# A state-space convolution with gated mixing: six additions moved from VectorE into accumulating transfers begun by GpSimd

## The chip, the cores and the metric

One Trainium2 chip, of which the kernel uses one core. A core has TensorE (PE in the profile; its weight loads are PEld), VectorE (DVE), ScalarE (ACT), GpSimd (POOL) and SyncE (SP), each with its own queue of instructions, worked off in order, and 16 DMA engines that all queues share. The metric is the device time of one launch in microseconds; lower is better. Inputs and the output are bfloat16, of 2048 rows and 512 channels.

## What is computed

The reference, cut to what matters:

```python
# A: a state-space convolution over L = 2048 positions, for each of 512 channels
dt = exp(log_dt); logdA = dt * (A_re + 1j*A_im)
P  = exp(logdA[:, :, None] * l)                    # 128 states, 2048 lags
K  = einsum("dn,dnl,dn->dl", C, P, dt*B).real      # kernel of lags
y  = irfft(rfft(pad(u)) * rfft(pad(K)))[:, :L] + u * Dskip
# B: two rows of x, chosen by the largest x @ w_r, go through a gated feed-forward
#    and are added back to those rows
b  = x + scatter(two rows, sigmoid(r) * ((silu(x_sel @ w_gate) * (x_sel @ w_up)) @ w_down))
# mix
g  = sigmoid((x * gate_w).sum(-1))
out = g * y + (1 - g) * b
```

## The kernel before

**Lags.** The kernel of lags needs exp(logdA * l) for 2048 lags. A lag is split into a coarse and a fine part, t1 + t2, and a table is built for each: the coarse table (`coarse`, tile TP: 32 lags, real and imaginary) and the fine table (`fine`, tiles X and Y in TQ: 20 lags and 8 more). Each is an exponential decay times a cosine or a sine of a phase; ScalarE makes the decays and the sines, VectorE multiplies. The channels are worked in two halves of 256, called half 0 and half 1. TensorE then sums over the states (`lags`: matmuls L889 and L890, evictions `kae`, a selection matmul L903, and the evictions `kce` and `kcx` into the tile KC).

**The fine table of one half** (`fine`, L840 to L859) goes through VectorE in steps of 2048 or 4096 columns per partition. For each of two groups of four lags: `px` (one product into X), `py` (the other product into a scratch tile `t4` at A+22528), `ps` (X += `t4`). Group k = 0 is lags 0 to 3, group k = 1 is lags 4 to 7. Then two wide products `px` and `py` for lags 8 to 15, from group 0, and for the last four lags again `px`, `py` into the same scratch place, `ps`. The scratch place `t4` is one range of bytes for all three sums of a half.

**Transforms.** The input U goes through a forward transform (`transform`, L729; TensorE L716) in two blocks m = 0, 1 of 1024 positions and two planes pl (real, imaginary). The matmuls of one tile first sum the odd rows, which are evicted doubled (`fwo`), then go on summing the even rows, so that the same bank then holds the sum of both (`fwe`). The difference, the spectrum's other half, is `fwe - fwo`: `vb` (L739), one VectorE operation of 2048 columns for each block and plane, four in all. The `vb` results are read only by the products of spectra (`products`, L952), late in the kernel.

**Spectra and inverse.** `spectrum` (TensorE L930, L932, L935) turns KC into the spectrum KH of the lag kernel, evicted by ScalarE (`khe`). `products` multiplies on VectorE, partly summed by TensorE (L993 to L997), and `inverse` (L1071, L1076) goes back to positions; evictions (L1087, L1091) scale by g, and the rows go out.

**The routed rows.** Beside all this, small steps (`rows`) find the two rows, gather them, run the feed-forward on TensorE (L779, L795 is the down projection `dn`, which reads `hh`, made by GpSimd) and scatter two rows into a copy of the input in DRAM (`sc`, L812, an indirect transfer begun by GpSimd, which needs `bu`). GpSimd also does the small steps of the gate: `sgd`, `sgo`, `gf`, `gc`, `omg`, and last `rr` (L814), which waits for the reciprocal `rrec` (L813) on VectorE. `rr` is read by `rd` (L1127): eight scalings of the identity matrix on ScalarE (L1131), used by the inverse for the share 1 - g.

**What sets the order.** Every step is an entry of a program (`Prog.add`) with its engine, the tiles it reads and writes, and a cost. `add` gives each step the steps it must wait for: the writers of what it reads, and the writers and readers of what it overwrites, in other tiles too that share bytes (`b.overlaps()`). The order is written out by hand in `PLAN`, a list of (step, engine choice); each engine's queue is that list with only its own steps. The costs play no part when the list is replayed. At run time a step waits on semaphores: one counter for each engine, and one of its own for each DMA, which reaches its count when the data has landed. A step that waits holds up everything behind it in its engine's queue.

**Names for the numbers of the list.** `vb`: 106 and 97 (block 0), 183 and 192 (block 1). Half 0's fine table: 258 `px`, 259 `py`, 260 `ps` (group k = 1), 263 `px`, 264 `py`, 265 `ps` (last four lags), 262 and 261 the wide products. Half 1's: 368 `px`, 369 `py`, 370 `ps` (k = 1), 373 `px`, 374 `py`, 375 `ps`, 372 and 371 wide; 367 is a sign change of half 1 (`nz`), 366 another (`nf`). 153 is `rrec`, 152 `sc`, 154 `rr`, 315 `rd`, 290 and 293 the evictions `kce`, 292 `kcx`, 144 `hh`.

VectorE's queue around them: 244, 245, 259, 367, 260, 264, 251, 265, 252, 261, then coarse steps of half 1, 363, 365, 153, 369, 373, 370, 290, 374, 366, 375, 372, 371, then 106, 97, the products of spectra with 183 and 192 among them. GpSimd's: 51, 77, 78, 84, 86, 55, 57, 58, 59, 80, 60, 82, 83, 140, 142, 143, 144, 152, 154. ScalarE's, late in the lags: 182 (`fwe` of block 1), 396, 286, 288, 315, 292, 293.

Of the kernel before, what the change touches and what calls it, by code (L numbers as in the profile page):

```python
# [15 lines left out]
ALU = mybir.AluOpType  # L16
# [290 lines left out]
def bass_gated_mix__ssm_conv_s4__moe_arch_mod__prompt_kernel(nc, A_u, A_A_re, A_A_im, A_B_re, A_B_im, A_C_re, A_C_im, A_log_dt, A_Dskip,  # L307
# [36 lines left out]
    with ExitStack() as es:  # L344
# [7 lines left out]
        P = Prog()  # L352
# [29 lines left out]
        def c_act(n):  # L382
            return 0.10 + n * 0.83e-3
# [17 lines left out]
        def f_act(o, a_, scale=1.0):  # L401
            return lambda h: h.activation(out=o(), in_=a_(), func=ACTF.Copy, scale=scale() if callable(scale) else scale)  # L402
# [12 lines left out]

        def DMA(name, fn, rd, wr, kb, n=1, eng=SP, issue=0.5, lat=2.2, **kw):
            return P.add(name, [(eng, issue, fn)], rd, wr, dma=(lat, kb / 270.0, n), **kw)

        def DMAT(name, o, a_, wr, kb, issue=1.25, lat=4.2, first=0.0):
            return P.add(name, [(SP, issue, lambda h: [h.dma_start_transpose(out=o(), in_=a_())])], [], wr, dma=(lat, kb / 250.0, 1), first=first)  # L420
# [288 lines left out]
        def forward(m, pl, kp, behind):  # L709
            t = P.pst(2, "fw", (0, 2))  # L710
            def product(par):
                def fw(h):
                    x = None
                    for k2 in range(2):
                        for i, (q, r) in enumerate((q, r) for q in range(2) for r in (par, par + 2)):
                            x = h.matmul(P32(t, k2, 0, 128, 0, (1, 512)), FM(0, 128, pl * 4096 + (par * 4 + i) * 512 + (2 * kp + k2) * 128, (1, 128)), U(0, 128, ((m * 2 + q) * 4 + r) * 512, (1, 512)),  # L716
                                         start=(par == 1 and i == 0), stop=(par == 0 and i == 3), skip_group_check=True)
                    return x
                MM("fw", fw, [bU[m][par], bF[pl]], [t], 1.73, behind=behind)
            def store(hc):  # L720
                o = lambda: V(0, 128, vo[m][2 * kp] + (hc * 2 + pl) * 512, (2048, 2), (1, 512))
                a = lambda: P32(t, 0, 0, 128, 0, (1, 1024))
                if hc == 0:
                    EV("fwe", o, a, [t], [bV[m][0][pl]], 1024)
                else:
                    P.add("fwo", [(ACT, c_act(1024), f_act(o, a, 2.0)), (DVE, c_dve(1024, 1), lambda h: h.tensor_scalar(out=o(), in0=a(), scalar1=2.0, scalar2=None, op0=ALU.mult))], [t], [bVO[m][pl]])  # L726
            return product, store

        def transform(m, behind=()):  # L729
            P.part = "transform%d" % m  # L730
            for pl in range(2):
                tiles = [forward(m, pl, kp, behind) for kp in range(2)]
                for hc in (1, 0):
                    for product, store in tiles:
                        product(hc)
                    for product, store in tiles:
                        store(hc)
                v = lambda hc, pl=pl: (lambda: V(0, 128, vo[m][0] + (hc * 2 + pl) * 512, (vo[m][2] - vo[m][0], 2), (2048, 2), (1, 512)))
                TT("vb", v(1), v(0), v(1), ALU.subtract, [bV[m][0][pl], bVO[m][pl]], [bV[m][1][pl]], 2048)  # L739
        transform(0)  # L740


# [97 lines left out]
        def fine(hf):  # L840
            P.part = "fine%d" % hf
            X, Y, Z, W, N, T = eX[hf], eY[hf], eZ[hf], eW[hf], eN[hf], el("A", 22528)
            bx = bX[hf]
            x = lambda j, n_, c=0, st=5120: ap(X + 5120 * c + 256 * j, (st, 2), (256, n_), (1, 256))
            t4 = ap(T, (1024, 2), (256, 4), (1, 256))
            for k, (j0, b0) in enumerate(((0, 4), (4, 0))):
                bt = bf_("t%d_%d" % (j0, hf), "A", 22528, 4096)
                TT("px", x(j0, 4), ap(W + 256, (256, 2), (0, 4), (1, 256)), ap(Z + 512 * b0, (0, 2), (512, 4), (1, 256)), ALU.mult, [bW[hf], bZ[hf][k]], [bx[k]], 2048)
                TT("py", t4, ap(W, (256, 2), (0, 4), (1, 256)), ap(Z + 512 * b0 + 256, (0, 2), (512, 4), (1, 256)), ALU.mult, [bW[hf], bZ[hf][k]], [bt], 2048)
                TT("ps", x(j0, 4), x(j0, 4), t4, ALU.add, [bx[k], bt], [bx[k]], 2048)  # L850
                if k == 0:
                    TS("nf", ap(N, (1, 256)), ap(X + 5120, (1, 256)), -1.0, ALU.mult, [bx[0]], [bNF[hf]], 256, 4)
                    TS("nz", ap(N + 256, (1, 256)), ap(Z + 512 * 8 + 256, (1, 256)), -1.0, ALU.mult, [bZ[hf][2]], [bNZ[hf]], 256, 4)
            TT("px", x(8, 8), ap(X, (5120, 2), (0, 8), (1, 256)), ap(Z, (0, 2), (512, 8), (1, 256)), ALU.mult, [bx[0]] + bZ[hf][:2], [bx[2]], 4096)
            TT("py", ap(Y, (2048, 2), (256, 8), (1, 256)), ap(N, (X - N, 2), (0, 8), (1, 256)), ap(Z + 256, (0, 2), (512, 8), (1, 256)), ALU.mult, [bx[0], bNF[hf]] + bZ[hf][:2], [bY[hf]], 4096)
            bt = bf_("t16_%d" % hf, "A", 22528, 4096)
            TT("px", x(16, 4), x(0, 4), ap(Z + 512 * 8, (0, 2), (0, 4), (1, 256)), ALU.mult, [bx[0], bZ[hf][2]], [bx[3]], 2048)
            TT("py", t4, x(0, 4, 1, -5120), ap(N + 256, (Z + 512 * 8 - N, 2), (0, 4), (1, 256)), ALU.mult, [bx[0], bNZ[hf], bZ[hf][2]], [bt], 2048)
            TT("ps", x(16, 4), x(16, 4), t4, ALU.add, [bx[3], bt], [bx[3]], 2048)  # L859
# [350 lines left out]
```

## Time and profile before

| | us |
|---|---|
| median of 3 runs (lowest to highest) | 158.67 (158.35 to 159.69) |
| the profiled execution's own time | 159.26 |
| its span, first to last instruction | 157.2 |
| TensorE busy (share of the span) | 140.8 (90%) |
| VectorE busy | 137.9 (88%) |
| ScalarE busy | 119.0 (76%) |
| GpSimd busy | 21.0 (13%) |

The span is what the trace covers; the execution's own time holds some 2 us around it. Busy times are unions of an engine's instructions; a matmul's end is modelled, so a busy TensorE is not one at its peak. The rows of a timeline give start, length, engine, line, operation, the tiles written and read, and their shapes; in brackets stands how long the engine was idle before and what ended the wait. All tiles in on-chip memory are views of one tensor, RB, and all banks are psm; most VectorE operations are recorded at the helper's line L386, so a step is told by its place in the queue and its size.

### The profile page before, as it was taken

To read this page: it belongs to the slowest core of one execution; us is meant where nothing else is said; L and a number is where in the kernel's file an instruction comes from. 1 tells how busy PE (TensorE), PEld (TensorE's weight loads), DVE (VectorE), ACT (ScalarE), POOL (GpSimd) and SP (SyncE) were. 2 spreads that over 40 slices of the span, in tenths; PEclk is the share of its full clock that TensorE was granted. 3 is DMA by queue.
4 is the path that set the end of the run, shared out by engine and by line. 5 is a ranking of instruction groups with operands and counts; after the bars stand their busy time and mean duration, and the time that the engine had idled before them with its cause. 6 is when DMAs were issued, how large, how long until landed. Compare 5 with 4: busy or idle time off the path is not lost.

```text
span 157.2 us, 3769 instructions
## 1 busy us (share of the span) xinstructions
PE 140.8 (90%) x1622; PEld 103.5 (66%) x1635; DVE 137.9 (88%) x184; ACT 119.0 (76%) x177; POOL 21.0 (13%) x26
## 2 busy tenths in 40 slices
PE   2479998999998999999967999999999999999960
PEld 0259976444764555778636899668877767777850
DVE  0799689999998999999999999999987999996930
ACT  5699999999999898887982754758687963567820
POOL 5000011564508800002020000000000000000000
PEclk9999999999999999999999999999999999999996
DMA  3999999968399000340397500558000040000157
GB/s 84 216 245 272 314 424 409 407 233 254 103 364 559 17 0 4 81 190 1 65 363 259 152 8 4 179 163 264 15 4 0 0 133 0 6 0 0 33 159 212
DMA packets 20932, 24.35 MB, mean 155 GB/s; under 512 B 9358, under 2 KB 18068, under 8 KB 20244
## 3 DMA queue, kind: packets, MB, share of 16 engines
q1 hardware_dynamic: 20642, 23.97, 47.3%
q8 instruction: 13, 0.21, 0.6%
q10 hardware_dynamic: 146, 0.13, 0.3%
q0 software_dynamic: 128, 0.01, 0.2%
q14 instruction: 3, 0.02, 0.0%
HBM read 19.78 MB, written 4.20 MB: 153 GB/s over the span
## 4 chain that ended last, share of the span: by engine, by line
PE 53%; DVE 32%; issue 4%; POOL 3%; ACT 2%; DMA 1%; POOLq 1%; ACTq 0%
DVE RB L386 23%; PE psm L930 9%; PE psm L1076 9%; PE psm L993 5%; PE psm L889 4%; PE psm L995 3%; PE psm L548 3%; PE psm L997 3%; PE psm L932 2%; PE psm L1071 2%; POOL RB L396 2%; PE psm L935 2%; DVE RB L726 2%; DVE RB L408 2%; PE psm L598 2%
## 5 line engine op out<-in xcount | busy, mean ns | idle before, releaser
L386 DVE TENSOR_TENSOR RB<-RB 128x2048 bf16<-128x2048 bf16 (+5 forms) x112 | 110.0, 1033 | 2.4 <-ACT RB L402 1.1
L402 ACT ACTIVATE RB<-psm 128x1024 bf16<-128x1024 f32 (+5 forms) x54 | 49.1, 945 | 23.7 <-PE psm L997 10.0
L716 PE MATMUL psm<-RB 128*128 128x512 bf16 x121 | 28.8, 379 | 1.2 <-ACT RB L402 0.5
L411 ACT ACTIVATE RB<-RB 128x512 bf16<-128x512 f32 (+6 forms) x48 | 27.0, 644 | 1.7 <-DVE RB L386 1.5
L411 ACT ACTIVATE RB<-psm 128x1024 bf16<-128x1024 int16 (+2 forms) x23 | 21.6, 968 | 2.5 <-DVE RB L386 1.2
L716 PEld LDWEIGHTS psm<-RB 128*128 128x128 bf16 x128 | 11.7, 97 | 14.0 <-ACT RB L402 1.1
L1076 PE MATMUL psm<-RB 128*128 128x256 bf16 x128 | 18.9, 273 | 0.0
L889 PE MATMUL psm<-RB 128*128 128x80 bf16 x256 | 16.5, 197 | 0.0
L890 PE MATMUL psm<-RB 128*128 128x32 bf16 x256 | 16.4, 177 | 0.0
L889 PEld LDWEIGHTS psm<-RB 128*128 128x128 bf16 x256 | 16.1, 96 | 0.2
L890 PEld LDWEIGHTS psm<-RB 128*128 128x128 bf16 x256 | 16.0, 96 | 0.2
L930 PE MATMUL psm<-RB 128*128 128x256 bf16 x128 | 14.5, 273 | 1.5 <-ACT RB L402 1.5
L930 PEld LDWEIGHTS psm<-RB 128*128 128x128 bf16 x128 | 12.4, 98 | 3.9 <-ACT RB L402 2.1
L1076 PEld LDWEIGHTS psm<-RB 128*128 128x128 bf16 x128 | 12.5, 98 | 1.5
L408 DVE CAST RB<-psm 128x1024 bf16<-128x1024 f32 (+3 forms) x8 | 8.6, 1080 | 3.7 <-PE psm L548 1.7
L993 PE MATMUL psm<-RB 128*128 128x512 bf16 x35 | 11.3, 379 | 0.3
L1087 ACT ACTIVATE RB<-psm,RB 128x256 bf16<-128x256 f32 x25 | 9.8, 477 | 1.3 <-PE psm L1076 1.1
L396 POOL CAST RB<-RB 128x16 bf16<-128x16 f32 (+4 forms) x6 | 7.2, 1197 | 24.8 <-DVE RB L405 16.9
L618 PE MATMUL psm<-RB 128*128 128x256 f16 x64 | 9.0, 272 | 0.0
L1071 PE MATMUL psm<-RB 128*128 128x256 bf16 x32 | 8.7, 273 | 0.0
L995 PE MATMUL psm<-RB 128*128 128x256 bf16 x40 | 8.3, 272 | 0.1
L997 PE MATMUL psm<-RB 128*128 128x256 bf16 x40 | 8.3, 273 | 0.0
(74 smaller groups left out, 156.9 us busy)
## 6 DMA issues: line engine op xcount, KB each, us to landing
RB<-c_fwd SPq DMA_DIRECT2D x2, 1024.0 KB, 7.9
RB<-in_A_u_dram SPq DMA_DIRECT2D x2, 1024.0 KB, 6.8
RB<-c_near SPq DMA_DIRECT2D x2, 1024.0 KB, 5.2
RB<-u_routed SPq DMA_DIRECT2D x2, 1024.0 KB, 5.1
RB<-in_B_w_up_dram SPq DMA_DIRECT2D x1, 1792.0 KB, 10.4
RB<-in_B_w_gate_dram SPq DMA_DIRECT2D x1, 1792.0 KB, 14.4
RB<-in_B_w_down_dram SPq DMA_DIRECT2D x1, 1792.0 KB, 8.7
out_dram<-RB SPq DMA_DIRECT2D x6, 256.0 KB, 3.0
```

The lines of the kernel that those rows point to most:

```text
L386: return P.add(name, [(eng, c_dve(n, mode) if eng == DVE else 1.6, lambda h: h.tensor_tensor(out=o(), in0=a_(), in1=b_(), op=op))], rd, wr ...
L402: return lambda h: h.activation(out=o(), in_=a_(), func=ACTF.Copy, scale=scale() if callable(scale) else scale)
L411: return P.add(name, [(ACT, cost or c_act(n), lambda h: h.activation(out=o(), in_=a_(), func=func, scale=scale))], rd, wr, table=table, **kw)
L716: x = h.matmul(P32(t, k2, 0, 128, 0, (1, 512)), FM(0, 128, pl * 4096 + (par * 4 + i) * 512 + (2 * kp + k2) * 128, (1, 128)), U(0, 128, ((m ...
L889: h.matmul(P32(t, q // 6, 0, 128, (q % 6) * 80, (1, 80)), tp, TQv(0, 128, c * 10240 + ri * NT2 * 256 + r * 4, (256, NT2), (1, 4)), start=( ...
L890: x = h.matmul(P32(t, q // 6, 0, 128, (q % 6) * 80 + 32, (1, 32)), tp, ARENA(0, 128, eY[c] + ri * 2048 + r * 4, (256, 8), (1, 4)), start=F ...
L930: x = h.matmul(o, KN(0, 128, g * 2048 + col, (1, 128)), KC[c](0, 128, g * 256, (1, 256)), start=(g == 0), stop=(g == NG - 1))
L993: r = h.matmul(P32(t, kt, 0, 128, 0, (1, 512)), CI(0, 128, 0, (1, 128)), f(k, 0, 512), start=(k == 0 and hc == 1), stop=False, skip_group_ ...
L995: r = h.matmul(P32(t, kt, 0, 128, 256, (1, 256)), CI(0, 128, 0, (1, 128)), f(k, 0, 256), start=False, stop=False, skip_group_check=True)
L997: r = h.matmul(P32(t, kt, 0, 128, 0, (1, 256)), NEG(0, 128, 0, (1, 128)), f(k, 1, 256), start=False, stop=(k == od[-1]), skip_group_check= ...
L1071: h.matmul(o, RD(0, 128, (tb + 8) % 16 * 128, (1, 128)), UE[q](0, 128, r * 256, (1, 256)) if early else U2(0, 128, tb * D + c * CW, (1, 25 ...
L1076: x = h.matmul(o, G(0, 128, (pl * 2 + kt // 2) * 1024 + (r * 2 + q) * 128, (1, 128)), PQ(0, 128, r * 1024 + kt * 256 + pl * 256 if quarter ...
```

## The change

Six VectorE operations become transfers that add while they write. A new helper `ACC` makes a step of GpSimd that begins one transfer for each pair of views: out += in, both in on-chip memory. Its numbers (1.5 us for each issue, 4.0 us and 100 KB per us for the landing) are costs of the list's search and don't act when the list is replayed.

- The four `vb` become `ACC` steps of two transfers each (one for each pair of columns blocks, 256 KB each). As a transfer adds and doesn't subtract, `fwo` is now evicted times -2 in place of 2, on either engine.
- `ps` of group k = 1, once for each half, becomes an `ACC` step of one transfer (512 KB). The other two `ps` of each half stay on VectorE.
- In the list, the `vb` stand right behind their last eviction (106 behind 104, 97 behind 95, 183 behind 182, 192 behind 191), 260 right behind 259 (and so ahead of 367), and 370 right behind 369 (ahead of 373).

By this list GpSimd's queue becomes: ..., 59, **106**, 80, 60, 82, 83, 140, 142, 143, **260**, **97**, 144, **192**, **370**, **183**, 152, 154. The queues of TensorE, ScalarE and SyncE keep their order, and VectorE's keeps its own without the six. What a step waits for follows from the tiles as before.

```diff
@@ the list, cut to the places that move
-..., (102, 0), (104, 0), (202, 0), ...
+..., (102, 0), (104, 0), (106, 0), (202, 0), ...
-(93, 0), (177, 0), (259, 0), (367, 0), (260, 0), (264, 0), (246, 0), (247, 0), (95, 0), (317, 0), ...
+..., (93, 0), (177, 0), (259, 0), (260, 0), (367, 0), (264, 0), (246, 0), (247, 0), (95, 0), (97, 0), (317, 0), ...
-..., (273, 0), (191, 0), (332, 0), ...
+..., (273, 0), (191, 0), (192, 0), (332, 0), ...
-..., (153, 0), (369, 0), (373, 0), (370, 0), (278, 0), ..., (182, 0), (396, 1), ...
+..., (153, 0), (369, 0), (370, 0), (373, 0), (278, 0), ..., (182, 0), (183, 0), (396, 1), ...
@@
+        def ACC(name, vs, rd, wr, kb):
+            return P.add(name, [(POOL, 1.5 * len(vs), lambda h: [h.dma_start(out=o(), in_=a_(), accum_op=ALU.add) for o, a_ in vs])], rd, wr, dma=(4.0, kb / 100.0, len(vs)))
@@ forward, store
-                    P.add("fwo", [(ACT, c_act(1024), f_act(o, a, 2.0)), (DVE, ..., scalar1=2.0, ...)], [t], [bVO[m][pl]])
+                    P.add("fwo", [(ACT, c_act(1024), f_act(o, a, -2.0)), (DVE, ..., scalar1=-2.0, ...)], [t], [bVO[m][pl]])
@@ transform
-                v = lambda hc, pl=pl: (lambda: V(0, 128, vo[m][0] + (hc * 2 + pl) * 512, (vo[m][2] - vo[m][0], 2), (2048, 2), (1, 512)))
-                TT("vb", v(1), v(0), v(1), ALU.subtract, [bV[m][0][pl], bVO[m][pl]], [bV[m][1][pl]], 2048)
+                v = lambda hc, z, pl=pl: (lambda: V(0, 128, vo[m][2 * z] + (hc * 2 + pl) * 512, (2048, 2), (1, 512)))
+                ACC("vb", [(v(1, z), v(0, z)) for z in range(2)], [bV[m][0][pl], bVO[m][pl]], [bV[m][1][pl]], 512)
@@ fine
-                TT("ps", x(j0, 4), x(j0, 4), t4, ALU.add, [bx[k], bt], [bx[k]], 2048)
+                if k == 1:
+                    ACC("ps", [(x(j0, 4), t4)], [bx[k], bt], [bx[k]], 512)
+                else:
+                    TT("ps", x(j0, 4), x(j0, 4), t4, ALU.add, [bx[k], bt], [bx[k]], 2048)
```

More of the change, by code (lines that the diff above doesn't have):

```diff
@@ L725, in store @@
                 else:
-                    P.add("fwo", [(ACT, c_act(1024), f_act(o, a, 2.0)), (DVE, c_dve(1024, 1), lambda h: h.tensor_scalar(out=o(), in0=a(), scalar1=2.0, scalar2=None, op0=ALU.mult))], [t], [bVO[m][pl]])
+                    P.add("fwo", [(ACT, c_act(1024), f_act(o, a, -2.0)), (DVE, c_dve(1024, 1), lambda h: h.tensor_scalar(out=o(), in0=a(), scalar1=-2.0, scalar2=None, op0=ALU.mult))], [t], [bVO[m][pl]])
             return product, store
```

30 rows, old and new, of the table PLAN are left out of this document.

## The prediction

> **What bounds the kernel now.** I read the engines' shares first, then the windows by stage, then the chain of waits.
>
> ```profile
> span 157.2 us, 3769 instructions
> PE 140.8 (90%) x1622; PEld 103.5 (66%) x1635; DVE 137.9 (88%) x184; ACT 119.0 (76%) x177; POOL 21.0 (13%) x26
> 60.00:72.00 12.00, 11.82 (x161) 8.20 (x162) 11.93 (x13) 10.25 (x13) 0.00 (x0) 1.00 0.26 89
> 72.00:84.00 12.00, 9.50 (x214) 7.21 (x212) 11.76 (x12) 10.11 (x19) 2.15 (x2) 1.00 0.54 187
> 84.00:100.00 16.00, 16.00 (x330) 14.88 (x328) 15.70 (x12) 7.99 (x10) 0.00 (x0) 1.00 0.28 70
> 100.00:114.00 14.00, 14.00 (x143) 10.55 (x142) 13.42 (x16) 10.07 (x12) 0.00 (x0) 1.00 0.53 172
> 114.00:140.00 26.00, 25.73 (x198) 19.30 (x200) 24.60 (x31) 18.00 (x33) 0.00 (x0) 1.00 0.08 22
> 140.00:152.00 12.00, 11.92 (x100) 9.34 (x99) 8.40 (x15) 7.30 (x14) 0.00 (x0) 1.00 0.12 34
> ```
>
> The columns of a window are its length and then the busy time of PE, PEld, DVE, ACT and POOL. TensorE idles 2.50 us from 72 to 84, and only 0.35 us in the 68 us behind that. So from about 84 us on TensorE alone sets the end: whatever moves its start there moves the end by as much, and no relief of VectorE behind 84 us can be seen in the time. The same chain around that start:
>
> ```profile
> 72.92 1.07 POOL u_routed L812
> 73.99 4.71 issue
> 78.69 1.15 POOLq L344
> 79.86 2.45 ACT RB L1131 x8
> 82.34 0.60 ACT RB L402
> 82.96 0.61 ACT RB L402
> 83.61 0.39 PE psm L930 x2
> ```
>
> TensorE's long run starts at 83.61 with the spectrum products. They wait for two evictions on ScalarE (82.34 and 82.96), these stand behind the eight L1131 scalings (`rd`), and those wait for GpSimd's `rr`:
>
> ```profile
> 78.74 1.09 POOL L386 TENSOR_TENSOR RB<-RB 128x16 f32<-128x16 f32 x1 [4.75 <-DVE RB L813]
> ```
>
> `rr` waited 4.75 us, for the reciprocal `rrec` (L813) in VectorE's queue; the 4.71 us of "issue" are that wait. So the time is set by VectorE's row of work up to `rrec`, GpSimd's `rr`, ScalarE, and TensorE from 83.61 on, with no slack between them.
>
> **The change, part by part.** Taken from VectorE are six instructions of 2048 columns. Which ones lie ahead of `rrec`?
>
> ```profile
> 53.26 1.26 DVE L386 TENSOR_TENSOR RB<-RB 128x2048 bf16<-128x2048 bf16 x1
> 54.56 0.23 DVE L390 TENSOR_SCALAR RB<-RB 128x256 bf16<-128x256 bf16 x1
> 54.70 1.22 DVE L386 TENSOR_TENSOR RB<-RB 128x2048 bf16<-128x2048 bf16 x1
> 55.95 1.23 DVE L386 TENSOR_TENSOR RB<-RB 128x2048 bf16<-128x2048 bf16 x1
> 78.57 1.18 DVE L386 TENSOR_TENSOR RB<-RB 128x2048 bf16<-128x2048 bf16 x1
> 80.83 1.21 DVE L386 TENSOR_TENSOR RB<-RB 128x2048 bf16<-128x2048 bf16 x1
> ```
>
> By the written order these are `py` of the fine table of half 0 (ends 54.52), a sign change, the sum `ps` that is moved (54.70), the `py` of the last four lags behind it (55.95), half 1's `py` (78.57, ends 79.75) and half 1's moved `ps` (80.83). The four differences `vb` stand behind half 1's whole table. Only the first `ps` is ahead of `rrec`: its start-to-start time, 1.25 us, is all that VectorE gains on the path. The other five, some 5.7 us by the same spacing, lie beside TensorE's unbroken run, where they are worth nothing.
>
> **Term A, the wait behind half 0's sum.** The `py` at 55.95 overwrites the scratch tile that the sum reads. Before, both were on VectorE. Now that `py` waits until the transfer has landed, and VectorE's whole row to `rrec` stands behind it. The transfer is issued when the earlier `py` is done, at 54.6. How long it takes no row of this kernel shows, so it is put together from these:
>
> ```profile
> RB<-in_gate_w_dram POOLq DMA_DIRECT2D x1, 1.0 KB, 4.0
> RB<-in_A_u_dram SPq DMA_DIRECT2D x4, 32.0 KB, 2.0
> out_dram<-RB SPq DMA_DIRECT2D x6, 256.0 KB, 3.0
> RB<-c_far SPq DMA_DIRECT2D x1, 512.0 KB, 7.9
> ...
> DMA  3999999968399000340397500558000040000157
> ```
>
> A transfer of 1 KB begun by GpSimd lands after 4.0 us. For the data I take the output rows, whose runs are 512 bytes like those of the table: (3.0 - 2.0) us over 224 KB, 4.46 ns per KB. An accumulation reads both operands, 2 x 512 KB, which makes 4.6 us. Together 8.6: it lands at 63.2, and the second `py` starts 7.25 us late. The ends are 4.0 us (no time for data; A = 2.65) and 11.9 us (4.0 and all of the 7.9 us that 512 KB took among other loads; A = 10.55). A gain is excluded: that needs a landing within 1.35 us of the issue. I stay with 8.6, near the output rows, since the DMA engines are idle then: the last row gives their busy tenths in slices of 3.93 us, and slices 14 to 16 (51 to 63 us) are 0.
>
> The Trainium skill, "DMA: Bandwidth & Descriptors", section "Anatomy of one DMA — SWDGE (gpsimd) path", gives 2.0 us and the bytes at 436 GB/s for such a transfer. By that an estimate for 512 KB is 3.2 us, A would be 1.85 and the time 168.2; the 4.0 us of the 1 KB row speak against its fixed part.
>
> **Term B, GpSimd's queue ahead of `rr`.** In the new order `rr` stands behind half 1's `ps` (one transfer), one `vb` (two transfers) and the scatter. Half 1's `ps` waits for the `py` that ends at 79.75, and that one is behind `rrec`: `rr`, which could follow `rrec` at once, now waits for later VectorE work and for all these issues.
>
> ```profile
> L505 POOL DMA_DIRECT2D RB<-in_gate_w_dram x1 | 1.0, 1007 | 0.4 <-issue 0.4
> L505 POOL DMA_DIRECT2D RB<-in_B_w_r_dram x1 | 0.8, 788 | 0.0
> 76.56 1.02 ACT L402 ACTIVATE RB<-psm 128x1024 bf16<-128x1024 f32 x1
> ```
>
> The last row is the eviction that this `vb` reads; it ends at 77.58, before the queue gets there. Counted without term A: 79.75, then 1.01 + 1.01 + 0.79 for three issues, 1.07 for the scatter (its row at 72.92 stands above), 1.09 for `rr` and about 0.3 for handing over end at 85.0, against 79.83 before. B = 5.2. The ends: three issues of 0.79 and no handing over, 4.5; and an issue held up by VectorE, which one row shows:
>
> ```profile
> 46.83 3.55 POOL L396 CAST RB<-RB 128x1 bf16<-128x1 f32 x2 [5.07 <-DVE RB L663]
> 46.69 3.40 DVE L386 TENSOR_TENSOR RB<-RB 128x4096 bf16<-128x4096 bf16 x2
> ```
>
> Two casts of one column took 3.55 us, as long as two wide VectorE operations beside them. One such issue in three adds 2.3 us: B = 7.5. I take 5.2, because the scatter issued beside VectorE's multiplications at 72.92 took only its 1.07.
>
> The Trainium skill, "SBUF — State Buffer", section "Who interferes with whom", says that GpSimd cannot write its descriptors while VectorE runs in a mode that takes both port pairs, and that a two-input operation blocks only GpSimd's reads. By that rule the issues here would be held up only by sign changes; the casts, which read, agree with it, and no issue in this trace lies under a long operation.
>
> **Term C, a cold TensorE.** Before 83.61 TensorE idled 1.53 us. With B it idles at least 5 us more. The start of this kernel shows what a pause does:
>
> ```profile
> 8.70:11.20 2.50, 2.49 (x12) 1.79 (x13) 2.50 (x9) 2.50 (x6) 0.00 (x0) 1.00 1.27 290
> 12.00:14.00 2.00, 2.00 (x9) 1.81 (x8) 2.00 (x7) 1.98 (x4) 0.00 (x0) 1.00 1.27 290
> 14.00:16.00 2.00, 2.00 (x19) 2.00 (x18) 1.44 (x5) 1.99 (x3) 0.00 (x0) 1.00 1.17 219
> 83.60:90.70 7.10, 7.09 (x67) 6.37 (x68) 7.10 (x6) 2.85 (x3) 0.00 (x0) 1.00 0.61 173
> 154.00:157.00 3.00, 0.00 (x0) 0.00 (x0) 0.00 (x0) 0.00 (x0) 0.00 (x0) 0.54 0.74 208
> ```
>
> After the first pause a 256-column matmul came every 0.21 us (12 in 2.50), against 0.106 at 83.6 (the clock column says 1.00 in both), and the rate doubled only near 14 us. The granted clock also falls to 0.54 some 3 us after the last matmul. Half speed for 5 us costs 2.5 us. The ends are 0 (the clock holds) and 2.8.
>
> **What is hidden.** The first `vb` pushes three small GpSimd steps back by 2 us; GpSimd idles 5.07 us behind them, as the casts' row shows. For the rest:
>
> ```profile
> 57.47 0.29 PE L795 MATMUL psm<-RB 128*128 128x2 bf16 x6 [0.19 <-ACT RB L402]
> 60.50 2.29 DVE L386 TENSOR_TENSOR RB<-RB 128x4096 bf16<-128x4096 bf16 x1
> 65.23 0.20 PE L889 MATMUL psm<-RB 128*128 128x80 bf16 x1
> ```
>
> `hh`, which the down projection (57.47) needs, now follows one `ps` and one `vb` and is done near 54.6 + 2.8 + 1.1 = 58.5. TensorE is about 1 us late there. Term A covers it: the lag products at 65.23 need VectorE's wide `px` (60.50 to 62.79), which moves by A to 70.0. If A were near 2 us or less, this 1 us would show. Half 1's transfer lands at 79.8 + A + 8.6 = 95.7. Behind it VectorE has two operations of 1.2, two wide ones of 2.2 and a sign change, 7.0 us, over at 102.7; TensorE wants that table after its 64 spectrum matmuls, at 90.7 + A + B + C = 105.7. This is late only if the transfer takes over 11 us.
>
> **The sum**: 7.25 + 5.2 + 2.5 = 14.95 us. On the span that is 172.2, on the profiled execution's own 159.26 us it is 174.2. Its time lies 0.6 us above the median of the runs; on the median, 158.67 us, it makes 173.6. I predict that.
>
> **The rivals.**
> **Quick landing**: the accumulation adds almost nothing to the 4.0 us. For it: the DMA engines are idle then. Against: two operands of 512 KB. A = 2.65, the time 158.67 + 2.65 + 5.2 + 2.5 = 169.0; with the lower ends of B and C it is 165.9.
> **Held-up issue**: the issues on the path are as slow as the casts, 3.3 us instead of about 1. For it: the 3.55 us row. Against: VectorE itself waits at just those places, so little runs beside them. Three of them add 6.9 us: 180.5.
> **Relief reaches the path** (not slower): VectorE comes to `rrec` 1.25 us earlier. Place: 54.70; price: 158.67 - 1.25 = 157.4. It decides only where the landing takes under 1.35 us and `rr` finds GpSimd free. The 4.0 us row and the queue's order speak against both.
> **The wait isn't there**, so that the change does less than it says: then A falls to -1.25 and B + C remain, 165.1. Against: every writer of a tile is given its readers to wait for.
>
> **How the numbers follow.** The forecast (A from 5 to 10.5, so 170 to 178) has 0.66, quick landing 0.17, held-up issue 0.11, no wait 0.03, relief 0.03. The low ends, 2.65 + 4.5 + 0, make 165.9; the high ends, 10.55 + 7.5 + 2.8, make 179.5, and I add a little for the third rival: 166 to 181. About 1% is what a measurement of this kernel can tell from no change. Slower by over 1%: 0.96; within 1%, the relief and an unforeseen cancelling: 0.03; faster: 0.01.
>
> **What would show it.** For A: VectorE idle about 7 us near 55 to 63, ended by a DMA. For B: `rr` right behind the scatter and three issues, `rd` on ScalarE idle before it, and L930 starting near 96. For C: L930's first matmuls spaced 0.21 us. VectorE's busy time should fall by about 7 us with nothing to show for it. The prediction is wrong if VectorE does not wait at 55, if `rr` runs straight behind `rrec`, or if TensorE's run from L930 on is broken by new waits.

## The result and the profile after

| | before | after |
|---|---|---|
| median (lowest to highest), us | 158.52 (158.35 to 159.69), 4 runs | 174.18 (173.22 to 174.56), 4 runs |
| profiled execution, us | 159.26 | 173.22 |
| its span, us | 157.2 | 171.2 |

The ratio after to before is 1.0937 (95% interval 1.0849 to 1.1024). The prediction was 173.6 us, with a range of 166 to 181. A fifth run after the change took 172.1 us and is not in its median; with it the median is 174.12. Ratios here and below are taken from the runs within 1.5% of their kernel's fastest; of one kernel below, named there, that leaves out three of six. In the new kernel line numbers behind the added helper are 3 greater, those behind `fine` 6 greater: L930 is now L936, L716 is L719, L813 is L816, L1131 is L1137, L889 is L895.

The profile of the changed kernel, its engines' shares:

```profile
span 171.2 us, 3773 instructions
...
PE 144.3 (84%) x1622; PEld 104.8 (61%) x1635; DVE 131.5 (77%) x178; ACT 119.3 (70%) x177; POOL 31.3 (18%) x36
```

VectorE has 6 instructions and 6.4 us less (137.9 before), GpSimd 10 instructions and 10.3 us more. TensorE has as many matmuls as before and is busy 3.5 us longer: some of its work ran slower. The windows of the changed kernel by stage (length; busy PE, PEld, DVE, ACT, POOL; granted clock; DMA share; GB/s):

```profile
60.00:72.00 12.00, 7.54 (x39) 3.43 (x37) 10.58 (x10) 5.55 (x7) 0.00 (x0) 0.73 0.26 40
72.00:84.00 12.00, 11.88 (x231) 9.75 (x232) 9.73 (x12) 9.14 (x11) 2.45 (x2) 0.99 0.57 134
84.00:100.00 16.00, 8.16 (x131) 5.83 (x130) 7.82 (x9) 6.74 (x15) 4.87 (x5) 0.79 0.94 234
100.00:114.00 14.00, 14.00 (x312) 13.17 (x311) 11.67 (x8) 7.46 (x9) 0.00 (x0) 1.00 0.16 45
114.00:128.00 14.00, 14.00 (x144) 10.49 (x143) 11.58 (x13) 10.08 (x12) 0.00 (x0) 1.00 0.56 174
128.00:154.00 26.00, 25.73 (x197) 19.31 (x200) 24.26 (x30) 18.35 (x34) 0.00 (x0) 1.00 0.08 21
```

From 100 us on the stages are those of before, some 14 us later, and TensorE is again without a gap. The time was lost in two stretches, 60 to 72 and 84 to 100, each with idle TensorE and a granted clock below 1 (0.73 and 0.79). The chain of waits of the changed kernel in both (start, length, what):

```profile
54.62 6.77 DMA RB<-RB
...
61.42 2.36 DVE RB L386 x2
...
86.29 0.16 DVE RB L816
86.45 1.11 DVE RB L386
87.56 0.29 issue
87.86 3.64 POOL RB L420 x3
91.50 1.30 POOLq L344
92.80 0.03 issue
92.82 0.24 POOL RB L386
...
93.09 2.44 ACT RB L1137 x8
95.56 0.60 ACT RB L402
96.18 0.61 ACT RB L402
96.83 8.48 PE psm L936 x64
```

The first two rows are half 0's sum, a transfer of 6.77 us, and the second `py` behind it, which started at 55.95 before: term A is 5.47 us. The DMA engines were not idle under it. The copy of the input within DRAM, which SyncE begins at 41.3, landed after 13.2 us before the change, at 54.5, and now after 16.4, at 57.7 (the transfers of before, then of after; the last number is us from issue to landing):

```profile
u_routed<-in_A_u_dram SPq DMA_DIRECT2D x1, 13.2
```

```profile
u_routed<-in_A_u_dram SPq DMA_DIRECT2D x1, 16.4
```

Of what the change moved only the first `vb`, begun at 40.45, has data under way before 54.6, and with the four `vb` as the only transfers (below) the copy takes 16.3 us too. In the trace's landing records the sum comes in sixteen parts: thirteen from 59.57 to 59.92, the others at 60.40, 60.83 and 61.39, as the last three parts of the copy come late, at 57.10, 57.30 and 57.73. In all seven traces in which half 0's 512 KB are added by a transfer, the sum lands 3.6 to 3.7 us behind the copy. That its last parts wait for the copy, and that A would be up to 1.5 us shorter without it, is argued from these times; no run here takes the copy away.

In the chain, from 86.29 on stand `rrec`, half 1's `py`, the three issues, the scatter and `rr`, then ScalarE's scalings and TensorE's spectrum. The chain has only the end of `rrec`; by the timelines it starts at 86.21, 7.80 us later than before (78.41). `rr` ends at 93.06 in place of 79.83, 13.23 later: B, what was added between the two, is 5.43. L936 starts 13.22 later (83.61 before).

Between A and `rrec`'s 7.80 lie 2.33 us that the prediction doesn't have. The timeline of the changed kernel shows where they come from, in the brackets (how long the engine was idle and what ended it):

```profile
67.22 1.03 PE L623 MATMUL psm<-RB 128*128 128x256 f16 x4 [4.41 <-ACT RB L411]
68.70 3.59 PE L719 MATMUL psm<-RB 128*128 128x512 bf16 x8
...
73.31 1.03 ACT L411 ACTIVATE RB<-psm 128x1024 bf16<-128x1024 int16 x1 [2.53 <-PE psm L621]
...
76.23 0.43 DVE L628 TENSOR_SCALAR RB<-RB 128x1024 bf16<-128x1024 bf16 x1 [1.91 <-ACT RB L411]
```

VectorE's delay holds up ScalarE and through it TensorE, which idles 4.41 us. Its eight matmuls of L719 then take 3.59 us (1.90 before), the group behind them that ScalarE reads (L621) comes late, ScalarE waits 2.53 us for these and VectorE 1.91 us for ScalarE: the delay comes back to VectorE's row, longer. The windows of the changed kernel, cut at the steps of the granted clock, show why:

```profile
62.00:65.40 3.40, 0.81 (x4) 0.20 (x2) 3.40 (x4) 0.00 (x0) 0.00 (x0) 1.00 0.23 36
65.50:72.20 6.70, 4.98 (x17) 2.02 (x18) 6.70 (x7) 4.46 (x5) 0.00 (x0) 0.50 0.00 0
72.30:76.00 3.70, 3.70 (x94) 3.57 (x93) 2.02 (x2) 2.69 (x3) 0.45 (x1) 1.00 0.69 235
...
92.80:96.80 4.00, 0.00 (x0) 0.00 (x0) 0.00 (x0) 3.63 (x10) 0.23 (x1) 0.50 1.11 234
96.90:99.50 2.60, 2.60 (x13) 1.86 (x14) 1.71 (x3) 0.00 (x0) 0.00 (x0) 0.50 1.13 161
99.60:105.30 5.70, 5.70 (x57) 5.12 (x56) 5.09 (x3) 2.85 (x3) 0.00 (x0) 1.00 0.41 110
```

In each pause the clock falls to 0.50 and stays there for some time under the matmuls that follow: from 65.4 to 72.3 and from 92.7 to 99.6. In the second stretch a matmul of L936 takes 0.20 us, then 0.10. Its 64 take 8.48 us instead of 7.16: C is 1.32.

**The account of the profiled pair**: 5.47 (A) + 2.33 (first slow stretch) + 5.43 (B) + 1.32 (C) = 14.55; the last matmul ends 14.54 later, and what follows it is 0.5 us shorter, which makes the 14.0 us of the spans. The medians are 15.7 apart, since the profiled run of before lay 0.7 above its median and that of after 1.0 below. No trace here divides up these 1.7 us.

### The profile page after: what moved, and what is told of

It is laid out like the page before. It is cut to its first block, busy times and chain, and to the rows that moved or that the text cites. A ratio compares the mean times of both kernels' runs of the same rounds, so it can differ in the third digit from the quotient of the medians.

```text
span 171.2 us, 3773 instructions
## 1 busy us (share of the span) xinstructions
PE 144.3 (84%) x1622; PEld 104.8 (61%) x1635; DVE 131.5 (77%) x178; ACT 119.3 (70%) x177; POOL 31.3 (18%) x36
## 4 chain that ended last, share of the span: by engine, by line
PE 56%; DVE 25%; DMA 5%; ACT 4%; POOL 4%; issue 1%; POOLq 1%; ACTq 0%
DVE RB L386 18%; PE psm L936 9%; PE psm L1082 8%; PE psm L999 5%; PE psm L895 5%; DMA RB<-RB 4%; PE psm L719 3%; PE psm L1001 3%; PE psm L1003 3%; PE psm L551 2%; ACT RB L411 2%; POOL RB L420 2%; PE psm L938 2%; PE psm L1077 2%; PE psm L941 2%; DVE RB L729 2%
## 5 line engine op out<-in xcount | busy, mean ns | idle before, releaser
L386 DVE TENSOR_TENSOR RB<-RB 128x2048 bf16<-128x2048 bf16 (+6 forms) x106 | 103.3, 1024 | 19.0 <-DMA RB<-RB 13.7
L719 PE MATMUL psm<-RB 128*128 128x512 bf16 x121 | 30.5, 396 | 1.2 <-ACT RB L402 0.5
L936 PE MATMUL psm<-RB 128*128 128x256 bf16 x128 | 15.8, 287 | 6.9 <-ACT RB L402 6.9
L719 PEld LDWEIGHTS psm<-RB 128*128 128x128 bf16 x128 | 12.1, 100 | 14.9 <-issue 2.6
L936 PEld LDWEIGHTS psm<-RB 128*128 128x128 bf16 x128 | 13.1, 103 | 10.0 <-ACT RB L402 7.5
L1082 PE MATMUL psm<-RB 128*128 128x256 bf16 x128 | 18.9, 273 | 0.0
L420 POOL DMA_DIRECT2D RB<-RB x10 | 12.3, 1606 | 28.3 <-ACT RB L402 17.0
L895 PE MATMUL psm<-RB 128*128 128x80 bf16 x256 | 16.5, 197 | 0.0
L896 PE MATMUL psm<-RB 128*128 128x32 bf16 x256 | 16.4, 177 | 0.0
L895 PEld LDWEIGHTS psm<-RB 128*128 128x128 bf16 x256 | 16.1, 96 | 0.2
L896 PEld LDWEIGHTS psm<-RB 128*128 128x128 bf16 x256 | 16.0, 96 | 0.2
L1082 PEld LDWEIGHTS psm<-RB 128*128 128x128 bf16 x128 | 12.5, 98 | 1.5
L999 PE MATMUL psm<-RB 128*128 128x512 bf16 x35 | 11.3, 379 | 0.3
L623 PE MATMUL psm<-RB 128*128 128x256 f16 x40 | 7.4, 287 | 4.4 <-ACT RB L411 4.4
L621 PE MATMUL psm<-RB 128*128 128x256 f16 x64 | 9.0, 274 | 0.0
L1137 ACT ACTIVATE RB<-RB 128x128 bf16<-128x128 bf16 x16 | 4.9, 389 | 5.9 <-POOL RB L386 5.9
```

The source lines that it names most:

```text
L386: return P.add(name, [(eng, c_dve(n, mode) if eng == DVE else 1.6, lambda h: h.tensor_tensor(out=o(), in0=a_(), in1=b_(), op=op))], rd, wr ...
L420: return P.add(name, [(POOL, 1.5 * len(vs), lambda h: [h.dma_start(out=o(), in_=a_(), accum_op=ALU.add) for o, a_ in vs])], rd, wr, dma=(4 ...
L621: r = h.matmul(o, DGM(0, 128, d * 128, (1, 128)), HL(0, 128, z * 512 + hf * CW, (1, CW)), start=(u == 0 and z == 0 and i % 2 == 0), stop=F ...
L895: h.matmul(P32(t, q // 6, 0, 128, (q % 6) * 80, (1, 80)), tp, TQv(0, 128, c * 10240 + ri * NT2 * 256 + r * 4, (256, NT2), (1, 4)), start=( ...
L896: x = h.matmul(P32(t, q // 6, 0, 128, (q % 6) * 80 + 32, (1, 32)), tp, ARENA(0, 128, eY[c] + ri * 2048 + r * 4, (256, 8), (1, 4)), start=F ...
L936: x = h.matmul(o, KN(0, 128, g * 2048 + col, (1, 128)), KC[c](0, 128, g * 256, (1, 256)), start=(g == 0), stop=(g == NG - 1))
```

## The experiments

Two theories stood after the traces. **Theory 1**: the four terms lie in a row, and each part taken back gives its terms. **The second wall**: half 1's table, which waits for its own transfer, is so late that work before it could come sooner without the end following. By the trace of after it is close behind: that transfer landed at 97.77, the table was ready at 104.69, and TensorE came for it at 105.3.

**Half 0's sum back on VectorE.**

```diff
-                if k == 1:
+                if k == 1 and hf == 1:
@@ the list
-(259, 0), (260, 0), (367, 0), (264, 0)
+(259, 0), (367, 0), (260, 0), (264, 0)
```

> The changed kernel with half 0's sum (`ps`, 260) back on VectorE in its old place. Theory 1 (the costs add up: a wait of 5.5 us behind that sum, 2.3 us of slow TensorE clock that follows from it, 5.4 us of GpSimd's queue ahead of `rr`, 1.3 us of slow clock at L936): the first two go, so 174.2 - 7.8 = 166.4, or a little less; VectorE goes without a gap from 53 us to `rrec`. Theory 2 (the waits overlap, and the queue ahead of `rr` alone sets the time): no change, 174.

Measured: 166.24 us (164.88 to 166.48), ratio 1.0445 (1.0388 to 1.0502). The chain of waits of this run has `rrec` back in its place, and GpSimd's queue as the only wait left:

```profile
78.24 0.16 DVE RB L816
...
79.80 2.44 POOL RB L420 x2
...
84.80 0.24 POOL RB L386
```

`rrec` ends at 78.40, and `rr` at 85.04, 5.2 us later than before the change. So half 0's sum costs 7.9 us (174.18 less 166.24), as theory 1 had it: A and the first slow stretch together are 7.80. This takes the sum away whole; it doesn't tell its wait for the copy from its own time.

**`rr` ahead of the transfers.** The scatter 152 and `rr` move from behind 371 to right behind `rrec` (with 151, a copy on SyncE that keeps its place in that queue).

```diff
-(153, 0), (369, 0), (370, 0), (373, 0), ..., (183, 0), (396, 1), (151, 0), (267, 0), ..., (371, 0), (152, 0), (154, 0), (315, 1)
+(153, 0), (151, 0), (152, 0), (154, 0), (369, 0), (370, 0), (373, 0), ..., (183, 0), (396, 1), (267, 0), ..., (371, 0), (315, 1)
```

> The changed kernel with the scatter and `rr` ahead of half 1's sum (370) and the last `vb` (183) in GpSimd's queue; both sums stay transfers. If the queue ahead of `rr` is all that holds L936 there: 174.2 - 5.4 - 1.3 = 167.5. If a second wall stands close behind it (half 1's `py`, 374, waits for the landing of 370, and the lag products of half 1 wait for VectorE's table, which was ready at 104.7 where TensorE came at 105.4): only the 0.7 us between the two are won, 173.3, and TensorE then idles in front of half 1's lag products in place of L936.

Measured: 174.71 us (173.59 to 175.17), ratio 1.0984 (1.093 to 1.1039). Nothing is won; theory 1's number is refuted, and the second wall's 173.3 lies 1.4 us too low. The timeline of this run:

```profile
86.07 1.09 POOL L386 TENSOR_TENSOR RB<-RB 128x16 f32<-128x16 f32 x1 [4.75 <-DVE RB L816]
...
97.41 1.23 DVE L386 TENSOR_TENSOR RB<-RB 128x2048 bf16<-128x2048 bf16 x1 [6.96 <-DMA RB<-RB]
...
104.46 0.23 PE L895 MATMUL psm<-RB 128*128 128x80 bf16 x1 [6.36 <-DVE RB L386]
```

`rr` runs straight behind `rrec`, and the spectrum ends 7.2 us earlier (98.10 in place of 105.31). Then TensorE idles 6.36 us before the lag products L895, for VectorE waited 6.96 us for half 1's transfer; and the clock falls to 0.50 in that pause, at 102.5, instead of before the spectrum, so that the lag products run at 0.50 up to 109.3. The second wall is there, and it stands under 1 us behind the first.

**Half 1's sum back on VectorE, alone and with `rr` ahead.**

```diff
-                if k == 1:
+                if k == 1 and hf == 0:
@@ the list; the second kernel also has the move of the run before
-(369, 0), (370, 0), (373, 0)
+(369, 0), (373, 0), (370, 0)
```

> The changed kernel with half 1's sum (370) back on VectorE; `rr` still stands behind the last `vb` (183) and the scatter. That `vb` can be issued when ScalarE's eviction ends (85.4) and takes 2.9 us, the scatter 1.3: `rr` ends near 90.0 in place of 93.06, TensorE idles 3 us less. Theory 1: 174.2 - 3.1 and some of the slow clock at L936 (up to 1.3): 170 to 171. Theory 2 (the queue alone sets the time, through half 1's sum): 174.2 - 5.4 = 168.8 or less.

> Half 1's sum (370) back on VectorE and the scatter and `rr` ahead of the last `vb` (183): only half 0's sum and the four `vb` are transfers, and none stands ahead of `rr`. Theory 1: only the wait behind half 0's sum and the slow clock that follows from it remain, 158.5 + 7.8 = 166.3; L936 no longer starts at the slow clock. Theory 2 (that wait is covered by others): 158.5 to 160.

Measured: alone 170.76 us (169.8 to 172.11), ratio 1.0734 (1.0687 to 1.078); with `rr` ahead 166.07 us (165.31 to 167.31), ratio 1.0442 (1.0399 to 1.0486). By the medians both fit theory 1 (170 to 171, and 166.3). In the waits of the first, then of the second kernel (us in total, times, longest), what TensorE waits for before the spectrum:

```profile
PE psm L936 <- ACT RB L402: 3.8, 1, 3.8
```

```profile
PE psm L936 <- ACT RB L402: 1.5, 1, 1.5
```

6.93 us after the change, 3.8 with one `vb` still ahead of `rr`, 1.5 (as before the change) with nothing ahead. In the first kernel L936 then takes 10.06 us (8.48 after the change), for the slow clock lasts from 93.1 to 99.9 there, and 6.0 us of it lie under L936: C is not a constant. Without half 1's transfer there is no second wall, and B and C go: 8.1 us below the changed kernel, by the medians; in the trace they are 6.75, and no trace shows what makes the rest. What is left, 7.3 us over the 158.80 of before measured beside it, is half 0's sum alone. The two parts taken back, 7.9 and 8.1 us, make 16.0 against the 15.7 of the whole change: the terms do lie in a row.

**The four `vb` alone, behind `rr`.** No sum is a transfer (`if k > 1:`, which never holds, and 260 and 370 at their old places), with the move of `rr`.

> Only the four `vb` are transfers; both sums are back on VectorE, and the scatter and `rr` stand ahead of the last `vb`. VectorE has 4 x 1.14 = 4.6 us less to do, all of it behind 84 us, where TensorE runs without a gap. Theory 1 (nothing is won there): 158.5, within 0.5. The rival (VectorE's relief is felt, or the transfers' traffic is): 154 to 157, or above 160.

Measured: 158.19 us (157.4 to 159.33), ratio 0.9979 (0.9935 to 1.0023). The engines' shares of this run:

```profile
PE 140.8 (89%) x1622; PEld 103.6 (66%) x1635; DVE 133.7 (85%) x180; ACT 119.1 (76%) x177; POOL 28.8 (18%) x34
```

Two windows of the same run, which answer to those of before from 84 to 114 us:

```profile
84.00:100.00 16.00, 15.92 (x328) 14.89 (x329) 13.24 (x10) 7.55 (x10) 0.00 (x0) 1.00 0.47 116
100.00:114.00 14.00, 14.00 (x144) 10.49 (x143) 11.51 (x13) 10.08 (x12) 0.00 (x0) 1.00 0.58 174
```

VectorE is busy 4.2 us less than before, TensorE as long as before and without a gap: the relief is worth nothing, and the transfers cost nothing once nobody on the path stands behind them. It is the best of the versions here and can't be told from the kernel before.

**TensorE kept busy in its pauses.** All transfers stay; added steps that nobody reads, 19 matmuls of 512 columns behind step 188 and 30 behind 289, run where TensorE would idle. A second kernel has the later 30 alone.

```diff
+        def warm(bank, n):
+            t = P.pst(1, "warm")
+            def f(h, t=t):
+                r = None
+                for i in range(n):
+                    r = h.matmul(P32(t, 0, 0, 128, 0, (1, 512)), CI(0, 128, 0, (1, 128)), CI(0, 128, 0, (0, 4), (1, 128)), start=True, stop=True)
+                return r
+            MM("warm", f, [bCIA], [t], 0.22 * n)
+        warm(4, 19)
+        warm(1, 30)
```

> The changed kernel with matmuls added that nobody reads, in TensorE's two long pauses: 19 of 512 columns behind the products that end at 62.8, 30 behind the selection products (L909); about 0.216 us each, so that each ends before the pause does. If the slow clock is a cause of its own, 2.3 us in the first pause and 1.3 in the second come back: 174.2 - 3.6 = 170.6. If it is only a sign of the waiting: 174, or more where the added matmuls are in the way.

> The same with only the 30 matmuls in the second pause, ahead of L936. If the slow clock there costs what L936's length says (8.48 us against 7.16): 174.2 - 1.3 = 172.9. If it is only a sign: 174.

Measured: both 169.55 us (169.07 to 170.31), ratio 1.0696 (1.0653 to 1.0739); the later alone 172.21 us over six runs (169.93 to 173.41), ratio 1.0757 (1.0698 to 1.0817) from the fastest three. The six spread by 3.5 us, more than the effect looked for, so this kernel doesn't price the second slow stretch. The windows of the run with both:

```profile
62.50:66.70 4.20, 4.20 (x20) 1.70 (x18) 4.20 (x4) 0.87 (x1) 0.00 (x0) 1.00 0.05 9
66.90:72.00 5.10, 5.09 (x74) 3.69 (x75) 5.10 (x6) 4.63 (x6) 0.00 (x0) 1.00 0.28 59
94.50:101.60 7.10, 7.10 (x64) 6.15 (x64) 6.78 (x5) 2.85 (x3) 0.00 (x0) 1.00 0.70 136
```

The clock stays at 1.00, the 64 matmuls of the spectrum take 7.16 us, and `rrec` starts at 83.86. Counted from the second `py`, which starts at 61.11 here and 61.42 after the change, that is 22.75 us in place of 24.79 (22.46 before): 2.0 us of the first slow stretch come back. Of the 1.32 us that the spectrum gains, 0.23 are lost again. The chain of waits of this run goes through half 1's transfer and its table, and TensorE waits for that table (L896 there is L895 of the changed kernel):

```profile
85.50 9.30 DMA RB<-RB
```

```profile
101.87 0.20 PE L896 MATMUL psm<-RB 128*128 128x80 bf16 x1 [0.23 <-DVE RB L387]
```

The second wall stands here too (in the trace of the kernel with the later 30 alone TensorE waits 0.82 us at it), so what a warm TensorE could win at the second pause is capped. More work on TensorE made the kernel 4.6 us faster by the medians, 3.8 by the spans (167.4). The slow clock was a cause by itself, of 2.0 + 1.1 us in this trace.

**Half 0's sum with its readers later.** To see whether that wait can be hidden: as the run with half 1's sum back and `rr` ahead, and the second `py`, `ps` (264, 265) behind the wide products (261), 97 behind `hh` (144).

> Half 0's sum and the four `vb` are transfers, `rr` stands ahead of the last `vb`, `hh` ahead of the second `vb`, and VectorE does the steps 251, 252 and 261 before it comes to 264 and 265, which need the scratch place: independent work of 4.5 us lies in the landing of 6.8 us. Theory 1: VectorE still waits about 2.2 us (59.2 to 61.4), against the 1.2 us that it saves, so it is 1 us late at `rrec`: 159.5. The rival (reordering hides the landing and the relief reaches the path): 158.5 - 1.2 = 157.3.

Measured: 161.56 us (160.75 to 162.56), ratio 1.0185 (1.0138 to 1.0231), 2 us above the higher of the two expectations. The timeline of this run:

```profile
55.67 4.69 DVE L386 TENSOR_TENSOR RB<-RB 128x2048 bf16<-128x2048 bf16 x3 [1.65 <-ACT RB L402]
60.85 3.62 DVE L386 TENSOR_TENSOR RB<-RB 128x2048 bf16<-128x2048 bf16 x3 [0.50 <-DMA RB<-RB]
```

A window of the same run, at the start of the spectrum:

```profile
84.90:88.20 3.30, 3.30 (x17) 2.29 (x16) 3.30 (x4) 0.00 (x0) 0.00 (x0) 0.50 1.13 253
```

VectorE waits 0.50 us for the transfer in place of 6.83, and 1.65 us for an eviction that the old order had covered. Counted from half 0's first `py` (52.49 here, 53.26 before), `rrec` is 1.5 us late. TensorE idles 1.94 us before the spectrum (1.53 before), and the clock falls to 0.50 for 3.4 us, which neither theory had: the spectrum takes 8.83 us in place of 7.16. In this order the sum doesn't pay either; that it can in none, since it has only one instruction of 1.25 us to win, is argued and not shown.

**What the transfer costs.** Half the bytes in half 0's and half 1's sums, then the same 512 KB copied without the addition. Each leaves a product of those lags out of the table, so they serve the timing alone.

```diff
-                    ACC("ps", [(x(j0, 4), t4)], [bx[k], bt], [bx[k]], 512)
+                    ACC("ps", [(ap(X + 256 * j0, (1, 1024)), ap(T, (1, 1024)))], [bx[k], bt], [bx[k]], 256)
@@ in the other kernel
+                    P.add("ps", [(POOL, 1.5, lambda h, o=x(j0, 4): [h.dma_start(out=o(), in_=t4())])], [bx[k], bt], [bx[k]], dma=(4.0, 5.0, 1))
```

> The changed kernel whose two sums (260, 370) add only the real plane, 256 KB in place of 512; the imaginary plane of those four lags is left without its second product. What is read is the time from issue to landing at 54.6 us. By the prediction's working (4.0 us fixed, 8.9 ns per KB) 6.3 us; if the time is mostly the data's, with about 2 us fixed, 4.4 us. VectorE's wait and the slow clock behind it shrink by as much as the landing does: the time falls from 174.2 by 0.5 in the one case and by 2.4 or more in the other.

> The changed kernel whose two sums are plain copies of the second product, begun by GpSimd, of the same 512 KB: the first product of those four lags is left out of the table. If an accumulation pays for two reads: by the prediction's working 4.0 + 2.3 = 6.3 us to the landing, and well under the 6.77 of the accumulation. If the addition is free and the path alone costs: 6.8 us, and the time stays at 174.

Measured: 170.21 us and 169.34 us, one run each, beside 158.34 for before. The transfer in the chain of the first, then of the second:

```profile
54.81 4.38 DMA RB<-RB
```

```profile
53.77 4.80 DMA RB<-RB
```

From 256 to 512 KB the accumulation grows from 4.38 (4.4 was the second expectation) to 6.77 us. A line through the two has 9.3 ns per KB and 2.0 us that don't depend on the size, counted from the start of the issue. The same 512 KB without the addition take 4.80 us, 2.0 less than with it; both expectations for that kernel (6.3 and 6.8) were too high. None of these is a transfer's time by itself: in all three traces the copy of the input lands in between (57.7, 57.7 and 57.0), and two transfers of a `vb` are begun right behind. From the copy's landing on, the 512 KB with the addition take 3.7 us, 256 KB 1.5 and the plain 512 KB 1.6. So the size and the addition count, by one run each, and a fixed part of 2.0 us is not shown. The plain transfer's issue also held GpSimd for only 0.80 us; half 0's accumulating one took 1.23 in the run before.

## Where the prediction was right and where not

- **What bounds the kernel: right.** VectorE's row up to `rrec` and TensorE from L930 on set the time. The four `vb` as transfers took 4.2 us off VectorE and nothing off the end. Two slips of reckoning change nothing in the forecast: quick landing with the lower ends of B and C is 165.8, not 165.9, and five operations at 1.25 us make 6.25, not 5.7.
- **Term A: right in its place, 1.8 us too large** (7.25 forecast, 5.47 measured; the landing 8.6 against 6.77). The mis-sized term is the landing: 4.0 us taken as fixed from the 1 KB row and 4.6 us of data. Which of the two was too large stays open. The line through two sizes has 2.0 us and 9.3 ns per KB (8.9 forecast), but the premise that "the DMA engines are idle then" did not hold: the first `vb` had put off the copy of the input to 57.7, and the last parts of the sum came behind it. The text saw that this `vb` delays GpSimd's small steps, not that its data delays the loads. As far as that made the landing longer, it brought the measured time nearer to the forecast, by luck. The runs of bytes that move together turned out to be 2 KB (256 packets of 2 KB in the trace) and not the 512 bytes argued with. The Trainium skill's rule, which the text set aside ("DMA: Bandwidth & Descriptors", section "Anatomy of one DMA — SWDGE (gpsimd) path", 2.0 us and the bytes at 436 GB/s), does not fit this transfer beside its traffic: the wait estimated by it, 1.85 us, is a third of the one measured. Even the first part of the sum landed 4.95 us behind the issue, and from 57 to 61 us all transfers together moved 170 GB/s.
- **Term B: right** (5.2 forecast; 5.43 in the trace, 5.2 with half 0's sum back). Inside it two sizes differ and cancel: the three issues took 3.64 us, not 2.81, and `rr` 0.24, not 1.09.
- **Term C: right in kind, too large** (2.5 forecast, 1.32 measured). The clock had fallen at 92.7, during the pause, so only the last 2.7 us of the slow stretch lay under matmuls. The step that failed is that the slow time was counted from the first matmul. With half 1's sum back on VectorE the same step cost 2.90 us (10.06 less 7.16): the size hangs on where the stretch begins.
- **Left out: the first slow stretch, 2.33 us.** The text saw that A moves `px` and the lag products but priced only the wait. That TensorE pauses there too, and then is slow in work on which VectorE waits in turn, was missed. With A and C too large by 3.0 together it nearly cancels: the sum for the span was 14.95, the trace has 14.0. That the total came out closer than its terms is luck.
- **What is hidden: right.** TensorE waited 1.40 us at the down projection for `hh`, beside VectorE's longer wait for the transfer. Half 1's table was late "only if the transfer takes over 11 us": it took 9.9, and the table was ready 0.6 us ahead of TensorE. That this left no room to shorten B by itself was not seen; the run with `rr` ahead found it.
- **The rivals.** Quick landing (4.0 us whatever the size) is refuted by both sizes, 4.38 us for 256 KB and 6.77 for 512. Held-up issue: the issues took 1.2 us each, not 3.3. Relief on the path: it needed a landing within 1.35 us, and the landing took 6.77. No wait: refuted by VectorE's 6.8 us for the DMA.

## What to carry to other kernels

An operation moved to a transfer is paid by whoever comes next to its source or its target, so price the landing against the work that lies between, and count every issue that slips in front of an unrelated step in the queue of the engine that starts it. Look first whether the relieved engine bounds the stage at all: here five of the six operations lay beside an unbroken TensorE. Look also at what the transfer's bytes do to the loads beside it: here the first `vb`, harmless in the queues, put off a copy of the input by 3.2 us. And a pause of several microseconds put into TensorE can cost more than its length: here the clock came back only 5.0 and 2.7 us after the work did; where such a pause can't be avoided, matmuls that nobody needs can pay.

## What was not expected of the hardware

- **The slow clock comes in steps.** In the changed kernel both stretches at 0.50 last 6.8 us (65.4 to 72.3, 92.7 to 99.6), with half 0's sum read later one lasts 3.4, in the plain-copy run one lasts 10.2 (87.2 to 97.5), and matmuls running in them don't end them early. The Trainium skill, "TensorE: Matmul & The Clock Gate", section "Part 1: The HAM clock gate (the "warmup" mystery)", tells of a free-running window of some 3.4 us, idle in which TensorE goes to half its clock and busy in which it comes back; the lengths agree with it. In the run with half 0's sum read later TensorE had paused only 1.94 us just before, and in the plain-copy run the clock fell at 59.9 too, 2.6 us behind a pause of 0.96 us; no run here explains why it fell there.
- **A transfer that adds took more than twice as long as a plain one**: 3.7 us against 1.6 for the same bytes, both counted from the landing of the input's copy, the plain one from a single run. Beside other loads and `vb`, half 1's accumulation of as many bytes took 9.9 us from issue to landing (87.86 to 97.77).
- **A small GpSimd operation takes four times as long beside VectorE**: `rr` 1.09 us before, where half 1's `py` ran beside it, and 0.24 after, where VectorE waited.
